# Early loads regrouped, and another order of the filter and back steps, in a spectral and attention kernel

## The chip, the cores and the metric

The kernel runs on one core of a Trainium2 chip. The metric is the device time of one execution in microseconds (us). The profile is of one execution on the same kind of core, in which every instruction of the engines and every packet of the DMA engines has a time. The engines are PE (TensorE, the matmuls), ACT (ScalarE), DVE (VectorE), POOL (GpSimd) and SP (SyncE, which here only issues transfers). Each of them works through its own instructions in order.

## What is computed

Four layers follow one another, each added to its input x (2048 rows by 512 columns, bfloat16): a spectral filter, attention, the same filter, the same attention.

```python
def _A_ref(x, w_r, w_i):
    X = rfft2(x.astype(float32), axes=(-2, -1))
    X = X * (w_r + 1j * w_i)
    return irfft2(X, s=(S, D), axes=(-2, -1)).astype(bfloat16)
...
x = x + _A_ref(_layernorm(x), A_w_r, A_w_i)
x = x + _B_ref(_layernorm(x), B_wq, B_wk, B_wv, B_wo)   # attention, 32 heads of 16, one key and value head
x = x + _A_ref(_layernorm(x), A_w_r, A_w_i)
x = x + _B_ref(_layernorm(x), B_wq, B_wk, B_wv, B_wo)
```

## The kernel before

`full_kernel` (L1162) loads x in four quarters into `x_sb`, and between them the tables `PH`, `S1` and `C1`, all on SP's queue. Then it runs twice `spectral_layer` (L217) and `attention_layer`. The change is in the loads of `full_kernel` and in `spectral_layer`.

The spectral layer makes the two-dimensional transform of matrix products with tables of sines and cosines. It works on two halves h of the frequencies, 0 and 1, in these steps:

- `forward(k, h)` (L257) multiplies two row tiles of x, turned by transposes (L198) in the first layer, with half h of `PH`: the transform along the columns. ACT scales the result by the layer norm's factor, which DVE (`norm.stats`, L155, called by `feed`, L1211) and POOL (L161) make.
- `first(k, h)` (L268) multiplies with `C1`, `S1` and `S1N` (the negated `S1`, made by DVE at L1220), copies the result to `A1`, and stores it to DRAM (`D1`, L277).
- `cross1(g, h)` (L279) reads it back in another order into `A2` (L280).
- `filtered(j)` (L317), called f below, multiplies a part of `A2` with the table `G`, copies it by ACT to X (L326), and multiplies it on DVE with the weights `wr_sb` (L330) and `wi_sb` (L332). `joined()` (L337) makes Z of the two products (L342, L343); it is called inside the next `filtered`, between its two products. There are eight, j = 0 to 7; 0 to 3 belong to half 0, 4 to 7 to half 1, and f4 is the first that reads half 1 of `A2`.
- `back(j)` (L345), called b, multiplies Z with the tables `H1`, `H2`, `H2N`, copies the result to B1 and stores it to DRAM (`D2`, L355).
- `cross2(h, g)` (L357) reads it back into `B2` (L358): four transfers for each half. Those of half 0 are called x0 below.
- `along(q, h)` (L374, L379) and `last(t, h)` (L388) are the inverse transform along the columns, with the addition to x; at the end of the layer attention's first keys and queries are made (L450), and L425 is its last line.

The loops `for k in range(9 + behind)` (half 0) and `for k in range(9)` (half 1) interleave forward, first and cross1. Inside them `load(k)` (L235) puts the loads of the layer's weights and tables into the queues at a given step: `wr_sb` at step 3, `H2` at 4 and `H1` at 5 on POOL's queue, `wi_sb` at 6, `G` at 9 where it is not loaded yet. The order of instructions on PE, ACT, DVE and SP is that of the program inside `spectral_layer` (`tc.manual_schedule`); POOL's is not fixed, and its instructions run as early as their data and the tile framework's order allow. A transfer that waits on SP's queue holds up every transfer behind it. The first four readings of half 0 and the stores of `D1` and `D2` are all on this queue. `wr_sb` shares its memory with the keys `Kv` of the attention layer before it (`tag="wrkv"`), `wi_sb`, `H1` and `H2` lie in a pool that is opened for each spectral layer, in memory which attention's pools used before.

The order of filter and back steps (L361) was f0, f1, f2, b0, f3, b1, f4, b2, f5, b3, f6, b4, x0, f7, b5, b6, b7, in both spectral layers.

Of the kernel before, what the change touches and what calls it, by code (L numbers as in the profile page):

```python
# [11 lines left out]
P = 128  # L12
BF = mybir.dt.bfloat16
# [32 lines left out]
VCELLS = 128  # L46
LASTW = 6
NEGATE = 7
NORMED, NORMG = (1,), ((3,), (3,), (3,))
OUTK, LATE_AT = 2, 4  # L50
TWICE = ((7,), 8)
# [87 lines left out]
def tile_of(x, k):  # L139
    return x[:, k // 4, k % 4, :]  # L140
# [69 lines left out]
def rotate(nc, ps, c, s, sn, re_im, first):  # L210

    nc.tensor.matmul(ps, lhsT=c, rhs=re_im, start=True, stop=False, skip_group_check=True)  # L212
    nc.tensor.matmul(ps[:, 0:128], lhsT=s, rhs=re_im[:, 128:256], start=False, stop=False, skip_group_check=True)
    nc.tensor.matmul(ps[:, 128:256], lhsT=sn, rhs=re_im[:, 0:128], start=False, stop=True, skip_group_check=True)  # L214


def spectral_layer(nc, tc, tabs, ht, A_w_r, A_w_i, x_sb, bigp, pre, norm, att, feed, weights):  # L217
    C1, S1, S1N, PH, ident = (tabs[n] for n in ("C1", "S1", "S1N", "PH", "ident"))
    with tc.tile_pool(name="workA", bufs=2) as work, tc.tile_pool(name="tabA", bufs=1) as tabA, \
# [7 lines left out]
        wi_sb = tabA.tile([P, 16, 256], BF, name="wi_sb")  # L227
        H1, H2, H2N = (tabA.tile([P, 16, P], BF, name=f"tab_{n}") for n in ("H1", "H2", "H2N"))

        def tables(names):  # L230
            for name in names:
                if tabs[name] is None:
                    tabs[name] = ht.load(tabs["pool"], name)

        def load(k):  # L235

            if k == 3:
                nc.sync.dma_start(out=wr_sb, in_=A_w_r.rearrange("(p a) f -> p a f", p=P)[:, :, 1:NF])
            elif k == 6:
                nc.sync.dma_start(out=wi_sb, in_=A_w_i.rearrange("(p a) f -> p a f", p=P)[:, :, 1:NF])  # L240
            elif k == 9:
                tables(("G",))
            elif k == 4:
                ht.load(tabA, "H2", H2, eng=nc.gpsimd)
            elif k == 5:
                ht.load(tabA, "H1", H1, eng=nc.gpsimd)
            elif k == 19:
                tables(("CS", "PSC", "PSS", "hmask"))
            weights(k)
# [29 lines left out]
        def cross1(g, h):  # L279
            nc.sync.dma_start(out=A2[32 * g:32 * g + 32, h, :, :],  # L280
                              in_=D1[h, 4 * g:4 * g + 4, :, :].rearrange("t (a b) c -> (t a) b c", b=16))
# [3 lines left out]
        for k in range(9 + behind):  # L285
# [6 lines left out]
            at = k - behind  # L292
# [7 lines left out]
        for k in range(9):  # L300
# [5 lines left out]
            if k >= 4 and k % 2 == 0:  # L306
                cross1((k - 4) // 2, 1)
            if k == NEGATE:
                nc.vector.tensor_single_scalar(out=H2N, in_=H2, scalar=-1.0, op=ALU.mult)
        cross1(3, 1)  # L310
        load(19)
        G, CS, PSC, PSS = (tabs[n] for n in ("G", "CS", "PSC", "PSS"))
# [4 lines left out]
        def filtered(j):  # L317

            h, b4 = j // 4, 4 * (j % 4)
            hf = slice(128 * h, 128 * h + 128)  # L320
            X = work.tile([P, 4, 2, 128], BF, name="X", tag="X", bufs=3)
            for b in range(b4, b4 + 4, 2):
                ps = bank()
                for i in range(2):
                    rotate(nc, ps[:, i, :], G[:, 0, :], G[:, 1, :], G[:, 2, :], A2[:, h, b + i, :], i == 0)
                nc.scalar.copy(out=X[:, b - b4:b - b4 + 2, :, :], in_=ps.rearrange("p j (r f) -> p j r f", r=2))  # L326
            m1, m2 = (M[:, i, j % 4] for i in range(2))
            wrb = wr_sb[:, b4:b4 + 4, hf].unsqueeze(2).to_broadcast([P, 4, 2, 128])
            wib = wi_sb[:, b4:b4 + 4, hf].unsqueeze(2).to_broadcast([P, 4, 2, 128])
            nc.vector.tensor_tensor(out=m1, in0=X, in1=wrb, op=ALU.mult)  # L330
            joined()
            nc.vector.tensor_tensor(out=m2, in0=X, in1=wib, op=ALU.mult)  # L332
            products.append((j, m1, m2))
# [11 lines left out]
        def back(j):  # L345
            h, b4 = j // 4, 4 * (j % 4)
            for b in range(b4, b4 + 4, 2):
                ps = bank()
                for i in range(2):
                    rotate(nc, ps[:, i, :], H1[:, b + i, :], H2N[:, b + i, :], H2[:, b + i, :], Z[:, h, b + i, :], i == 0)  # L350
                if j == 7 and b > b4:
                    nc.vector.tensor_copy(out=B1[:, h, b:b + 2, :], in_=ps)
                else:
                    nc.scalar.copy(out=B1[:, h, b:b + 2, :], in_=ps)
                nc.sync.dma_start(out=D2[h, :, b:b + 2, :], in_=B1[:, h, b:b + 2, :])  # L355
# [2 lines left out]
            eng.dma_start(out=B2[:, h, 4 * g:4 * g + 4, :],  # L358
                          in_=D2[h].rearrange("(t a) b c -> t (a b) c", t=16)[4 * g:4 * g + 4].rearrange("t m c -> m t c"))

        for j in range(10):  # L361
            if j < 8:
                filtered(j)
            if j >= 7:
                joined()
            if j >= 2:
                back(j - 2)
            if j == 6:
                for g in range(4):
                    cross2(0, g, nc.sync)  # L370

# [789 lines left out]
@with_exitstack  # L1161
def full_kernel(ctx, tc, A_x, A_w_r, A_w_i, B_x, B_wq, B_wk, B_wv, B_wo, out):  # L1162
    nc = tc.nc
    const = ctx.enter_context(tc.tile_pool(name="const", bufs=1))
    x_v = A_x.flatten_outer_dims().rearrange("(p r t) d -> p r t d", r=R, t=T)
    x_sb = const.tile([P, R, T, 512], BF, name="x_sb")
    ht = Tables(nc)
    tabs = dict(pool=const, CS=None, PSC=None, PSS=None, hmask=None, G=None)
    tabs["ident"] = ht.load(const, "ident", eng=nc.scalar)
    for part in (slice(0, 2), slice(2, 4)):  # L1170
        nc.sync.dma_start(out=x_sb[:, 0, part, :], in_=x_v[:, 0, part, :])
    tabs["PH"] = ht.load(const, "PH")
    tabs["S1"] = tabs["C1"] = None
    for r in range(1, R):
        nc.sync.dma_start(out=x_sb[:, r, :, :], in_=x_v[:, r, :, :])
        if r < 3:
            for n in ("S1", "C1"):
                tabs[n] = ht.load(const, n, tabs[n], slice(8 * r - 8, 8 * r))
    mhalf = const.tile([P, 4], F32, name="mhalf")
    nc.gpsimd.memset(mhalf, -0.5)  # L1180
    tabs["S1N"] = const.tile([P, 16, P], BF, name="tab_S1N")
    wq_sb = const.tile([P, NC, D], BF, name="wq_sb")
    wk_sb = const.tile([P, NC, DH], BF, name="wk_sb")
    wka = const.tile([P, NC, 8, DH], BF, name="wka")
    wo_sb = const.tile([P, 4, D], BF, name="wo_sb")
    wv_sb = const.tile([P, NC, DH], BF, name="wv_sb")
    xn_sb = const.tile([P, R, T, 512], BF, name="xn_sb")
    lnpool = ctx.enter_context(tc.tile_pool(name="lnpool", bufs=1))
    bigp = ctx.enter_context(tc.tile_pool(name="bigp", bufs=6))
    out_v = out.flatten_outer_dims().rearrange("(p r t) d -> p r t d", r=R, t=T)  # L1190
    att = Attention(nc, tabs, const, bigp, lnpool, wq_sb, wka.rearrange("p c v d -> p c (v d)"), wv_sb, xn_sb)

    def weights(k):
        if k == 19:
            nc.sync.dma_start(out=wk_sb, in_=B_wk.rearrange("(c p) j -> p c j", p=P))
            nc.sync.dma_start(out=wv_sb, in_=B_wv.rearrange("(c p) j -> p c j", p=P))
            for v in range(8):
                nc.gpsimd.tensor_copy(out=wka[:, :, v, :], in_=wk_sb)
        elif k == 20:
            nc.sync.dma_start(out=wq_sb, in_=B_wq.rearrange("(c p) j -> p c j", p=P))  # L1200
            nc.sync.dma_start(out=wo_sb, in_=B_wo.rearrange("(g p) c -> p g c", p=P))

    def make_norm():
        return Norm(nc, lnpool, mhalf, x_sb, xn_sb)

    def store(k, eng=nc.sync):
        eng.dma_start(out=tile_of(out_v, k), in_=tile_of(x_sb, k))

    norm = make_norm()

    def feed(k, psum):  # L1211

        for t in (0, 1) if k == 0 else ():
            norm.stats(t, tile_of(x_sb, t))
        if k < 7:
            norm.stats(2 * k + 2, tile_of(x_sb, 2 * k + 2))
            norm.stats(2 * k + 3, tile_of(x_sb, 2 * k + 3))
        if k in (2, 5):
            part = slice(0, 8) if k == 2 else slice(8, 16)
            nc.vector.tensor_single_scalar(out=tabs["S1N"][:, part], in_=tabs["S1"][:, part], scalar=-1.0, op=ALU.mult)  # L1220

    feed.busy, feed.xT = True, []
    for layer in range(2):
        norm_in, norm_out = make_norm(), make_norm()
        spectral_layer(nc, tc, tabs, ht, A_w_r, A_w_i, x_sb, bigp, norm, norm_in, att, feed,
                       weights if layer == 0 else lambda k: None)
        feed = attention_layer(nc, tc, att, norm_in, norm_out, x_sb, wo_sb, None if layer == 0 else store)
        norm = norm_out
# [47 lines left out]
```

## Time and profile before

| what | us |
|---|---|
| three timed runs | 1409.14, 1414.59, 1416.40 (median 1414.59) |
| the profiled execution | 1412.01 |
| its span, first to last instruction | 1410.20 |
| first spectral layer, to its last line L425 | 0 to 96.2 |
| first attention layer | 96.3 to about 709 |
| second spectral layer | about 709 to 793.9 |
| second attention layer | 793.9 to the end |

PE is busy in 95%, ACT in 94%, DVE in 93% of the span; the mean granted clock of PE is 0.997 of full speed. The DMA engines moved 34.5 MB, most of it in the two spectral layers. A row of the timeline gives the start, the duration, the engine, the line, the operation, the tile written and the tiles read, and in brackets how long the engine had been idle before it and what ended this. A row of the chain of waits gives start, duration and what was waited for. An engine's name with a q is its queue of transfers, the row being the issue and not the transfer.

### The profile page before, as it was taken

To read this page: it belongs to the slowest core of one execution; us is meant where nothing else is said; L and a number is where in the kernel's file an instruction comes from. 1 tells how busy PE (TensorE), PEld (TensorE's weight loads), DVE (VectorE), ACT (ScalarE), POOL (GpSimd) and SP (SyncE) were. 2 spreads that over 40 slices of the span, in tenths; PEclk is the share of its full clock that TensorE was granted. 3 is DMA by queue.
4 is the path that set the end of the run, shared out by engine and by line. 5 is a ranking of instruction groups with operands and counts; after the bars stand their busy time and mean duration, and the time that the engine had idled before them with its cause. 6 is when DMAs were issued, how large, how long until landed. Compare 5 with 4: busy or idle time off the path is not lost.

```text
span 1410.2 us, 34818 instructions
## 1 busy us (share of the span) xinstructions
PE 1344.2 (95%) x14050; PEld 471.8 (33%) x14118; DVE 1310.5 (93%) x2271; ACT 1331.1 (94%) x1542; POOL 824.6 (58%) x483
## 2 busy tenths in 40 slices
PE   7799999999999999999997999999999999999998
PEld 6653232223222222222275422332222222222222
DVE  5679999999999999999966899999999999999997
ACT  5679999999999999999955899999999999999997
POOL 2125676667666667667610267666666666666664
PEclk9999999999999999999999999999999999999999
DMA  7700000000000000002064000000000000000000
GB/s 249 210 29 2 1 2 2 2 1 2 2 2 1 2 2 2 1 1 40 8 183 147 2 2 2 2 1 9 5 5 1 6 9 5 2 1 10 9 2 16
DMA packets 44770, 34.52 MB, mean 24 GB/s; under 512 B 10048, under 2 KB 42048, under 8 KB 44096
## 3 DMA queue, kind: packets, MB, share of 16 engines
q1 hardware_dynamic: 41632, 28.98, 7.2%
q8 instruction: 110, 1.80, 0.5%
q0 software_dynamic: 576, 2.10, 0.4%
q10 hardware_dynamic: 2400, 1.21, 0.3%
q14 instruction: 52, 0.43, 0.1%
HBM read 20.22 MB, written 10.49 MB: 22 GB/s over the span
## 4 chain that ended last, share of the span: by engine, by line
ACT 47%; PE 33%; issue 9%; DVE 7%; DMA 3%; POOL 0%; SPq 0%; DVEq 0%; ACTq 0%; POOLq 0%
ACT e L1077 46%; PE pv L866 13%; PE sc L911 11%; DVE ph L951 3%; PE aux L911 2%; PE ps L262 1%; DMA D<-A 1%; PE aux L450 1%; DVE ln_stats L155 1%; DVE ph L983 1%; PE ps L212 1%; DMA x_sb<-in_A_x_dram 1%; DMA B<-D 1%; PE pv L881 1%; PE aux L679 1%
## 5 line engine op out<-in xcount | busy, mean ns | idle before, releaser
L1077 ACT ACTIVATE e<-sc 128x1024 bf16<-128x1024 f32 x1328 | 1218.2, 1166 | 2.9 <-PE sc L911 2.9
L975 POOL TENSOR_TENSOR ph<-ph,step 128x1024 int32<-128x1024 int32 x404 | 762.8, 1891 | 413.1 <-DVE ph L983 293.0
L951 DVE TENSOR_SCALAR ph<-aux 128x512 uint16<-128x512 f32 x1440 | 904.0, 679 | 20.5 <-PE aux L911 15.9
L866 PE MATMUL pv<-ph,vaug 128*32 128x512 bf16 x4320 | 548.8, 386 | 0.7 <-POOL ph L975 0.3
L911 PE MATMUL sc<-QT,Kv 32*128 32x512 bf16 x2656 | 521.8, 380 | 23.5 <-ACT e L1077 16.2
L866 PE MATMUL pv<-e,vaug 128*32 128x512 bf16 x2656 | 483.9, 384 | 0.3 <-ACT e L1077 0.3
L911 PE MATMUL aux<-QT,Kv 32*128 32x512 bf16 x1440 | 455.8, 384 | 1.0 <-DVE ph L951 0.5
L911 PEld LDWEIGHTS <-Kv 32*128 32x128 bf16 x4096 | 183.4, 91 | 525.9 <-issue 517.6
L881 PE MATMUL pv<-wo_sb,zeros 128*32 128x512 bf16 x1200 | 257.8, 383 | 0.0
L866 PEld LDWEIGHTS <-vaug 128*32 128x32 bf16 x6976 | 147.6, 94 | 292.8 <-issue 281.6
L983 DVE TENSOR_SCALAR ph<-ph 128x2048 uint16<-128x2048 uint16 x316 | 216.5, 685 | 0.5
L161 POOL TENSOR_TENSOR ln_rstd<-ln_veps,mhalf 128x4 f32<-128x4 f32 x16 | 16.6, 1036 | 123.7 <-DVE ln_veps L160 123.6
L155 DVE BATCH_NORM_STATS2 ln_stats<-x_sb 128x6 f32<-128x512 bf16 x64 | 43.5, 680 | 28.1 <-ACT x_sb L413 19.4
L881 PEld LDWEIGHTS <-zeros 128*32 128x32 bf16 x1200 | 60.1, 94 | 1.9 <-issue 0.3
L781 DVE STREAM_TRANSPOSE oT<-pv 128x512 f32<-128x512 f32 x64 | 45.2, 707 | 9.2 <-PE pv L866 9.2
L184 ACT ACTIVATE Pk<-ps,ln_rstd 128x256 bf16<-128x256 f32 x64 | 26.8, 474 | 21.9 <-PE ps L262 19.0
L262 PE MATMUL ps<-tab_PH,xT 128*128 128x256 bf16 x256 | 35.3, 286 | 3.9 <-DMA tab_PH<-const_PH 3.0
L276 DVE CAST A<-ps 128x512 bf16<-128x512 f32 x28 | 19.2, 689 | 17.8 <-PE ps L214 17.8
L450 PE MATMUL aux<-xTa,wq_sb 128*128 128x512 bf16 x90 | 32.6, 384 | 2.8 <-issue 2.4
L803 POOL TENSOR_TENSOR on<-oT,rden 128x512 bf16<-128x512 f32 x30 | 31.7, 1056 | 2.0 <-DVE rden L807 1.8
L679 PE MATMUL aux<-wo_sb,ph 128*128 128x512 bf16 x72 | 26.1, 383 | 3.6 <-issue 2.1
L262 PEld LDWEIGHTS <-xT 128*128 128x128 bf16 x256 | 25.1, 102 | 8.1 <-issue 3.7
(109 smaller groups left out, 668.3 us busy)
## 6 DMA issues: line engine op xcount, KB each, us to landing
D<-A SPq DMA_DIRECT2D x32, 128.0 KB, 3.2
A<-D SPq DMA_DIRECT2D x16, 256.0 KB, 3.5
D<-B SPq DMA_DIRECT2D x32, 128.0 KB, 2.5
B<-D SPq DMA_DIRECT2D x12, 256.0 KB, 4.5
tab_H<-const_H POOLq DMA_DIRECT2D x4, 512.0 KB, 6.4
wr_sb<-in_A_w_r_dram SPq DMA_DIRECT2D x2, 1024.0 KB, 6.2
wi_sb<-in_A_w_i_dram SPq DMA_DIRECT2D x2, 1024.0 KB, 7.4
out_dram<-x_sb SPq DMA_DIRECT2D x15, 128.0 KB, 1.7
```

The source lines that it names most:

```text
L155: nc.vector.bn_stats(st, src)
L262: nc.tensor.matmul(ps[:, j, :], lhsT=xT[:, cc, 2 * k + j, :], rhs=PH[:, cc, 256 * h:256 * h + 256], start=(cc == 0), stop=(cc == NC - 1), ...
L450: self.nc.tensor.matmul(ps, lhsT=w(c), rhs=self.xTq[:, c, qc * 512:(qc + 1) * 512], start=(c == 0), stop=(c == NC - 1), skip_group_check=True)
L679: nc.tensor.matmul(ps, lhsT=OTs[qb][:, g4, kk * P:(kk + 1) * P], rhs=wo_sb[:, g4, :], start=first, stop=last, skip_group_check=True)
L781: end = clock.now(clock.FLIP, lambda: nc.vector.transpose(out=oT[:, par].rearrange("p b c -> p (b c)"), in_=pv), clock.last + clock.MM_END)
L866: nc.tensor.matmul(pv_tiles[gi][32 * i:32 * i + 32, :], lhsT=vaug[:, kc, j, :], rhs=es, start=((gi, i) not in started), stop=(left[gi, i] ...
L881: nc.tensor.matmul(pv_tiles[gi][32 * i:32 * i + 32, :], lhsT=att.zeros, rhs=wo_sb[:, 0, :], start=False, stop=False, skip_group_check=True)
L911: nc.tensor.matmul(out, lhsT=Kv[r, par, kc * P:(kc + 1) * P], rhs=QT[r, g, qb * 512:(qb + 1) * 512], start=True, stop=True, skip_group_che ...
L951: end = clock.now(clock.Z, lambda: nc.vector.tensor_scalar(out=z.bitcast(U16), in0=ps, scalar1=SCALE * LOG2E * 128.0, scalar2=127.0 * 128. ...
L975: nc.gpsimd.tensor_tensor(out=copy.bitcast(I32), in0=z.bitcast(I32), in1=step.to_broadcast([P, w // 2]), op=ALU.add)
L983: nc.vector.tensor_scalar(out=one.bitcast(U16), in0=z.bitcast(U16), scalar1=float(PHASE[1]), scalar2=None, op0=ALU.add)
L1077: nc.scalar.activation(out=e[:, 0:ng * 512], in_=sc[:, 0:ng, :].rearrange("p a b -> p (a b)"), func=ACT.Exp, scale=SCALE)
```

## The change

The early loads: `PH` comes in two halves, the first in its old place, the second behind all of x. In the first layer `wr_sb`, `wi_sb`, `H2` and `H1` are put into SP's queue at steps 3, 4, 6 and 8, `H2` and `H1` no longer into POOL's. In the second layer all four are put into SP's queue at step 0, ahead of the layer's first store. The order of the filter and back steps is written out as a string: b2 and b3 and the four readings of half 0 come ahead of f4, and a join of its own ahead of b3.

```diff
+STEPS = "f0 f1 f2 b0 f3 b1 b2 j3 b3 x0 f4 f5 f6 b4 f7 b5 j7 b6 b7"
...
+        first_layer = tabs["G"] is None
...
         def load(k):
 
-            if k == 3:
+            at = (3, 4, 6, 8) if first_layer else (0, 0, 0, 0)
+            if k == at[0]:
                 nc.sync.dma_start(out=wr_sb, in_=A_w_r.rearrange("(p a) f -> p a f", p=P)[:, :, 1:NF])
-            elif k == 6:
+            if k == at[1]:
                 nc.sync.dma_start(out=wi_sb, in_=A_w_i.rearrange("(p a) f -> p a f", p=P)[:, :, 1:NF])
-            elif k == 9:
+            if k == at[2]:
+                ht.load(tabA, "H2", H2)
+            if k == at[3]:
+                ht.load(tabA, "H1", H1)
+            if k == 9:
                 tables(("G",))
-            elif k == 4:
-                ht.load(tabA, "H2", H2, eng=nc.gpsimd)
-            elif k == 5:
-                ht.load(tabA, "H1", H1, eng=nc.gpsimd)
             elif k == 19:
                 tables(("CS", "PSC", "PSS", "hmask"))
             weights(k)
...
-        for j in range(10):
-            if j < 8:
+        for step in STEPS.split():
+            j = int(step[1])
+            if step[0] == "f":
                 filtered(j)
-            if j >= 7:
+            elif step[0] == "b":
+                back(j)
+            elif step[0] == "j":
                 joined()
-            if j >= 2:
-                back(j - 2)
-            if j == 6:
+            else:
                 for g in range(4):
                     cross2(0, g, nc.sync)
...
-    tabs["PH"] = ht.load(const, "PH")
+    tabs["PH"] = const.tile([P, 4, 512], BF, name="tab_PH")
+    ph = nc.inline_tensor(ht.host["PH"], name="const_PH").ap()
+    nc.sync.dma_start(out=tabs["PH"][:, :, 0:256], in_=ph[:, :, 0:256])
...
         if r < 3:
             for n in ("S1", "C1"):
                 tabs[n] = ht.load(const, n, tabs[n], slice(8 * r - 8, 8 * r))
+    nc.sync.dma_start(out=tabs["PH"][:, :, 256:512], in_=ph[:, :, 256:512])
```

## The prediction

> **What bounds the kernel now.** I read first the busy shares in forty slices. Slices of 35 us are full on PE, DVE and ACT except at 0 to 105 us, about 705 to 810 us and the last slice: between them the attention stages keep ACT busy, and the change touches no line of theirs. So only the two spectral stages (L217 to L425) count: 0 to 95 us ("S1") and 709 to 793 us ("S2"). In the chain of waits, S1 begins with a load:
>
> ```profile
> 2.12 9.83 DMA x_sb<-in_A_x_dram
> 11.97 0.70 DVE ln_stats L155
> ...
> 41.76 3.72 DMA D<-A
> 45.92 2.79 DMA tab_CS<-const_CS
> ...
> 61.96 3.51 DMA D<-B
> 65.54 3.42 DMA B<-D
> ```
>
> The reader is to see that transfers end four waits: the second quarter of x; the exchange of the second half of A through DRAM (the row naming tab_CS is the queue's place: f4's operand is A2, landed at 48.74); the store and the reading of the second half of B. The timeline shows what happens at the first wait and at f4, first in S1, then in S2:
>
> ```profile
> 2.31 0.76 POOL L135 DMA_DIRECT2D tab_H<-const_H  x1
> 11.97 0.69 DVE L155 BATCH_NORM_STATS2 ln_stats<-x_sb 128x6 f32<-128x512 bf16 x1 [4.47 <-DMA x_sb<-in_A_x_dram]
> ```
> ```profile
> 48.98 0.27 PE L212 MATMUL ps<-A,tab_G 128*128 128x256 bf16 x1 [1.17 <-DMA tab_CS<-const_CS]
> ```
> ```profile
> 746.53 0.37 PE L212 MATMUL ps<-A,tab_G 128*128 128x256 bf16 x1 [2.96 <-DMA A<-D]
> ```
>
> S2 waits longer, and its clock falls. Busy time by stretch (PE is the second number; the clock is the last but two):
>
> ```profile
> 43.39:46.80 3.41, 1.83 (x25) 1.74 (x26) 3.41 (x9) 1.93 (x5) 0.00 (x0) 1.00 0.73 201
> 67.28:70.69 3.41, 1.44 (x10) 0.91 (x11) 0.00 (x0) 1.03 (x2) 0.00 (x0) 1.00 1.08 295
> 70.69:74.10 3.41, 3.41 (x11) 1.51 (x10) 1.70 (x4) 2.32 (x5) 0.00 (x0) 0.50 0.88 278
> 743.12:746.53 3.41, 0.45 (x8) 0.29 (x6) 1.96 (x4) 1.32 (x3) 0.00 (x0) 1.00 0.74 227
> 746.53:749.94 3.41, 3.41 (x25) 2.89 (x26) 0.90 (x2) 1.75 (x3) 0.00 (x0) 0.50 0.06 13
> ```
>
> The halved stretches begin 675.84 us apart, 198 times 3.413 us: the clock is set on a fixed grid, and follows the stretch before: 1.44 us of PE work in 3.41 was too little, 1.83 was enough.
>
> **Part 1, the start (S1).** Gone from the first microseconds: H2 and H1, which POOL issues at 2.3 and 3.2. Their packets (256 of 4 KB at 0.165 us, over 16 DMA engines) take 2.64 us of each engine between 6.7 and 12.3. PH, 8 packets of 159 ns on each engine (1.27 us), becomes a half of 32 packets of 512 bytes, at the 27 ns that such packets take in wr_sb's load: 0.86 us. So 0.41 us goes there too. Of the sixteen parts of x's second quarter fourteen landed by 8.49, the last two at 10.71 and 11.95. If those two stay late: 11.95 - 2.64 - 0.41 = 8.9, a gain of 3.1. If they keep up, x lands near 7, and DVE is free of the first quarter's statistics at 7.5: a gain of 4.5. I take the middle, **3.8**.
>
> The Trainium skill, "DMA: Bandwidth & Descriptors", Latency and other measured facts, says that two of the engines are usually slow and guesses that POOL's descriptors do it; by that guess the gain would be 4.5, and the sum below 0.7 better. The row for it is only the two late parts.
>
> What is late next: DVE, nearly without a pause from 11.97 to 26 (sixteen statistics at 0.66 to 0.69, copies, the negated table). S1's and C1's first halves landed at 13.1 and 13.8, 1.2 and 1.8 after x in the same queue, so move with it; x's last quarter (17.6, needed at 22) has slack, and PH's second half (0.86 us of DMA, needed at 29.6) too. The weights and H now stand in SP's queue at steps 3, 4, 6 and 8, each an issue of 0.43 to 0.66 us, with the stores of A behind them. I cost this at nothing: the last exchange of half 0 was issued by 35.7 and f0 starts at 40.5; in the new order wr and wi (landing 6.1 and 6.7 apiece) are through by about 27, H and the last stores by 31. Without that cover each late microsecond is one on f0.
>
> **Part 2, the order of steps.** A step is 0.88 us on PE (12 matmuls), 0.96 on ACT (two copies), a filter 2 x 0.605 on DVE, its join 2 x 0.335. b2 and b3 now come before f4. PE takes b2 when Z2 is there (49.1) and b3 when Z3 is (50.4, its join now before m1 of f4), so f4 starts at 51.3 instead of 48.98. Its wait is gone, but DVE needs f4's copies, which now come at 53.1 instead of 50.74 and idles 2.8 us. From there DVE paces: four filters and joins, 7.5 us plus small waits, and Z7 is ready at 61.3 instead of 59.73. **b7 ends 1.6 to 1.7 us later in S1**, by the same list that gives the old order within 0.2 us. This is the edit's price where A2 was late by only 1.17.
>
> In S2 A2 came at 746.5, 10.2 us after f0 (S1: 8.2). b2 and b3 fit before that, so f4 starts about then, warm, and b7's last copy ends 22.75 us after f0, as in S1's list. f0 itself waited 0.51 and starts at 735.75, because the four loads, now ahead of every store of A, are through before the first exchange is due: Kv is last read at 706.2, H's tiles were free at 708.95, and 3 MB take 2 x 3.5 + 2.64 us, to about 720; that exchange is issued at 721.95. Last copy 758.5, instead of 760.48: 2.0 gained.
>
> **Part 3, the readings x0.** 1 MB in 1 KB packets (64 per engine at 47 ns, 3 us) were issued at 56.89 to 58.91, with the last stores of B behind them; the last store took 3.51 where the median is 2.5. In the new order they go out by 57.3 while b4's first store comes at 57.2: nothing is blocked, and the last store has a free queue. Bounds: no gain, or 1.0; I take 0.7 in S1. In S2, from the last copy to the first reading of B took 7.89 us, in S1 7.44; new 6.7, so 1.2 there.
>
> **The clock.** PE stood idle 2.09 us before L379 at 69.01, and the half clock after it cost S1 25.91 us from there to L425, against S2's 24.23: 1.7. In the new order PE reaches that wait 1.6 later and the reading comes 0.9 later, so the idle is about 1.4, below the 1.58 that the row with 1.83 had: 1.7 goes. S2's half clock is within its 2.0.
>
> The Trainium skill, "TensorE: Matmul & The Clock Gate", What's actually happening, lets the clock fall after a whole idle window. The row with 1.44 us of work speaks against it. By the page the new gaps of part 2 could cost nothing; by the row they can, which is a rival below.
>
> **The sum.** Start -3.8; S1 +1.6 - 0.7 - 1.7 = -0.8; S2 -2.0 - 1.2 = -3.2; together **-7.8 us**. The profiled execution took 1412.01 (span 1410.20), so it would take 1404.2. The three timed runs are 1409.14, 1414.59 and 1416.4; with the profiled one their median is 1413.3, and I give **1405.5** as the time, 9 under the median shown. About 0.5% (7.1 us) is what a measurement here can tell from no change, so the forecast lies just beyond that bound.
>
> **Rivals.**
> 1. *The small version.* The two late parts stay late (-3.1), the order's price in S1 stays whole and its clock still falls (+1.7), S2 gains only 2.0: -3.4, 1409.9. For it: the clock grid is met by chance, and why two DMA engines lag is not shown. Against: x0 does leave the stores' way. Chance 0.32.
> 2. *The clock falls in the filter stage.* New PE gaps: 1.9 us from f6 to b4, and 1.4 + 0.4 around b2; a stretch that holds them whole has 1.5 to 1.6 us of work, between 1.44 (fell) and 1.83 (kept). Price up to 1.7 in each stage: -7.8 + 3.4 = -4.4, 1408.9. Chance 0.10.
> 3. *Slower: the first forward step waits for both halves of PH.* They are one tile; if the wait goes by tile, PE stands until the second half lands: x's last quarter landed at 17.57, less 2.64 and 0.41, plus 0.86, is 15.4. The first matmuls of L262 start there, not at 8.91; those, the transposes and the second eight take 4.6, and the first rotation starts at 20.0, not 14.53: +5.5 in place of -3.8, in all +1.5, 1414.8. It decides once that landing is past 10.1: with 1.9 us of matmuls behind it, PE would come to its next transposes after 12.0, where it began them before. Against: the second forward step starts at 12.82 while ACT writes other slices of xT at 13.07, so waits follow slices. Chance 0.05.
> 4. *More.* Start -4.5, the stores -1.0 in S1, S2 -4.2: -11, 1402. For it: fourteen parts of x land early. Chance 0.08.
>
> The forecast has 0.45, with its own range of 1402.5 to 1408.5. **Range** 1400.5 to 1412: from the fourth rival with the timed runs' scatter to the second and first with it; left out are the slower case and the edges. **Chances**: beyond 0.5% faster (below 1407.5) four fifths of the forecast and the fourth rival, 0.36 + 0.08, with some runs of the first and second, 0.47; slower by over 0.5% only if the third is worse than priced, 0.04; within, 0.49.
>
> **What would show it.** Right: the second DVE wait for x ends near 8 and f0 starts near 36.7; b2 and b3 before f4 in both stages; DVE idle some 2.8 us before f4's first product in S1; f4 in S2 without a DMA wait and at full clock; the last store of B landing in 2.5 us. Wrong: the first L262 waiting for tab_PH past 10.1 us; a clock of 0.50 among f4 to b7; f0 waiting for A2; SP's stores of A in S2 issued later than 712.56 by more than a microsecond. The forecast fails mostly if the start gains little or the two stages' ends do not follow b7.

## The result and the profile after

Nine runs of the changed kernel have a median of 1406.32 us (1404.63 to 1408.3), nine of the kernel before 1413.68 (1409.14 to 1416.97): a ratio of 0.9953, 95% interval 0.9938 to 0.9968. The profiled execution after took 1406.89 (span 1405.1), that of before 1412.01: the two profiles are 5.1 us apart, the medians 7.4.

In the changed file the lines of the spectral layer stand one to five further down (L212 is L213, L262 is L266, L326 is L330, L379 is L384, L425 is L430). The chain of waits of the kernel after, first spectral layer (start, duration, what was waited for):

```profile
2.30 6.94 DMA x_sb<-in_A_x_dram
...
43.01 2.99 DMA D<-A
46.06 4.48 DMA A<-D
...
62.99 3.17 DMA D<-B
66.28 3.41 DMA B<-D
```

The same four transfers end the same waits. x landed 2.7 us earlier (9.24 for 11.95), but the last two rows end at 69.69, where the chain before ended its reading at 68.96: by then the new order of steps has cost more than was left of the early start. The timeline of the kernel after at these places:

```profile
9.26 0.69 DVE L156 BATCH_NORM_STATS2 ln_stats<-x_sb 128x6 f32<-128x512 bf16 x1 [1.76 <-DMA x_sb<-in_A_x_dram]
39.22 0.27 PE L213 MATMUL ps<-A,tab_G 128*128 128x256 bf16 x1 [0.76 <-DMA D<-A]
50.59 0.28 PE L213 MATMUL ps<-A,tab_G 128*128 128x256 bf16 x1 [0.26 <-DMA A<-D]
52.39 0.69 DVE L334 TENSOR_TENSOR M<-X,wr_sb 128x1024 bf16<-128x1024 bf16 x1 [3.18 <-ACT X L330]
69.74 1.05 PE L384 MATMUL ps<-tab_CS,B 128*128 128x256 bf16 x8 [1.87 <-DMA B<-D]
745.45 0.27 PE L213 MATMUL ps<-A,tab_G 128*128 128x256 bf16 x1
747.29 0.69 DVE L334 TENSOR_TENSOR M<-X,wr_sb 128x1024 bf16<-128x1024 bf16 x1 [2.80 <-ACT X L330]
```

Row two is f0, which now waits for a transfer; row three f4 in S1, four is DVE at f4's product; the sixth is f4 in S2, with no bracket: its wait of 2.96 is gone. The busy time by stretch, on the grid of the clock, around f4 in S1 and in S2:

```profile
51.96:55.38 3.42, 1.66 (x24) 1.41 (x22) 2.99 (x6) 2.36 (x5) 2.96 (x6) 1.00 0.77 254
...
744.86:748.28 3.42, 3.40 (x47) 3.06 (x44) 0.99 (x2) 3.10 (x8) 0.00 (x0) 1.00 0.46 153
748.28:751.69 3.41, 1.78 (x24) 1.68 (x24) 3.41 (x9) 2.06 (x5) 0.00 (x0) 1.00 0.62 185
```

From 17.8 us on, up to the last 1.5 us, no stretch is at half clock; before, two were, counted from 19.5 us on. Ahead of these times PE runs at half speed in both profiles. The clock column does not show it: it reads 1.00 at the start as well. The durations of eight equal matmuls of L266 do; in the kernel after:

```profile
14.51 1.92 PE L266 MATMUL ps<-tab_PH,xT 128*128 128x256 bf16 x8
17.88 1.04 PE L266 MATMUL ps<-tab_PH,xT 128*128 128x256 bf16 x8
```

This first rise of the clock came between 8.0 and 20.2 us in the fourteen profiles of this document. A stretch of the grid with 2.68 us of work (4.17 to 7.58) and the two after it did not raise the clock here. In the run with the old order in S2 alone (below), whose program in S1 is the changed kernel's, the grid lay otherwise: the stretch from 5.62 held 2.80 us of work, and full speed came behind it, at 9.03:

```profile
6.71 1.87 PE L267 MATMUL ps<-tab_PH,xT 128*128 128x256 bf16 x8 [0.61 <-DMA tab_PH<-const_PH]
9.14 1.04 PE L267 MATMUL ps<-tab_PH,xT 128*128 128x256 bf16 x8
```

Where the 5.1 us went, from the starts of the first L262 (L266) row of S2 and of the last matmuls of the layer:

| stretch | before | after | difference |
|---|---|---|---|
| start to the first matmul of S2 (S1 and attention) | 709.23 | 708.22 | -1.0 |
| from there to the last L425 (L430) matmuls | 83.20 | 79.30 | -3.9 |
| from there to the end of the span | 617.8 | 617.6 | -0.2 |

### The profile page after: what moved, and what is told of

Same layout as the page of the kernel before. It is cut to its first block, busy times and chain, and to the rows that moved or that the text cites. A ratio compares the mean times of both kernels' runs of the same rounds, so it can differ in the third digit from the quotient of the medians.

```text
span 1405.1 us, 34816 instructions
## 1 busy us (share of the span) xinstructions
PE 1341.5 (95%) x14050; PEld 470.6 (33%) x14118; DVE 1310.0 (93%) x2271; ACT 1330.8 (95%) x1542; POOL 822.7 (59%) x479
## 4 chain that ended last, share of the span: by engine, by line
ACT 48%; PE 33%; issue 9%; DVE 7%; DMA 3%; SPq 0%; POOL 0%; DVEq 0%; ACTq 0%
ACT e L1082 47%; PE pv L871 13%; PE sc L916 10%; DVE ph L956 3%; PE aux L916 2%; PE ps L266 2%; DVE ln_stats L156 1%; PE aux L455 1%; PE ps L213 1%; DMA B<-D 1%; DVE ph L988 1%; PE pv L886 1%; PE aux L684 1%; DMA x_sb<-in_A_x_dram 0%; DMA D<-B 0%
## 5 line engine op out<-in xcount | busy, mean ns | idle before, releaser
L185 ACT ACTIVATE Pk<-ps,ln_rstd 128x256 bf16<-128x256 f32 x64 | 26.8, 472 | 19.7 <-PE ps L266 15.2
L266 PE MATMUL ps<-tab_PH,xT 128*128 128x256 bf16 x256 | 35.3, 286 | 1.6 <-DVE oT L786 0.8
L213 PE MATMUL ps<-Z,tab_H 128*128 128x256 bf16 x64 | 15.1, 275 | 13.0 <-DVE Z L347 12.9
```

Of the source, the lines that this page charges most:

```text
L266: nc.tensor.matmul(ps[:, j, :], lhsT=xT[:, cc, 2 * k + j, :], rhs=PH[:, cc, 256 * h:256 * h + 256], start=(cc == 0), stop=(cc == NC - 1), ...
```

## The experiments

Two questions were open. First, which edits make the gain: the theory was that S2's part is the one that counts, and that S1's earlier start is lost again at the exchange of A; the rival was the prediction's own sum, with half of the gain from the start. Second, what decides that the clock falls.

All times are beside runs of the kernel before on the same chip, whose medians were 1413.56 (first four kernels), 1413.27 (next four), 1412.93 (next three) and 1412.62 (the last).

### One part of the change at a time

**The order alone** (loads as before):

```diff
-        for j in range(10):
+        for step in STEPS.split():
```

> The kernel before with the new order of steps alone, in both spectral layers; the loads stay as they were. Theory (the order costs where A2 is only a little late and gains where it is very late): in the first layer the last copy of b7 comes 22.8 to 23.3 us after f0 instead of 21.1, and the first reading of the second half of B about 1 us later than 69.0; in the second layer f4 no longer starts at half clock, b7's last copy comes about 2 us and the reading about 3 us earlier. In all -1 to -4 us, ratio 0.997 to 0.999. Rival (the order gains in both layers, because the four readings of half 0 leave the way of the last stores): the first layer's reading of B also comes earlier, in all -5 us or more. Second rival (the second layer's gain came from the loads): the second layer gains under 1 us and the whole is +0.5 to +2.

1407.54 us (1404.98 to 1407.9), ratio 0.9956, 0.9944 to 0.9968. The order alone gives nearly the whole gain: 6.0 us, where the theory had 1 to 4. S2 took 79.96 from its first matmul to its end, f4 there had no wait, and from 11 us on no stretch was at half clock in either layer:

```profile
746.76 0.27 PE L213 MATMUL ps<-A,tab_G 128*128 128x256 bf16 x1
```

In S1 the first reading of half 1 of B came at 69.68, 0.7 later than before, as the theory had it, although f0 started 2.9 earlier (37.61) with the loads unchanged. Part of what the theory missed is the clock: it is 1.0 in all five runs (see the end of this section).

**The early loads of S2 alone** (old order, PH whole, S1's loads as before):

```diff
+            elif k == 0:   # second layer only: wr_sb, wi_sb, H2, H1 on SP's queue
```

> The kernel before with the second spectral layer's four loads at step 0 on SP's queue, nothing else changed (the first layer's loads, H2 and H1 on POOL's queue among them, the old order). Theory (SP's queue was held up by stores behind wr_sb and wi_sb): f0 of the second layer loses its wait of 0.51 us, the second half of A2 lands about 8 to 9 us after f0 instead of 10.2, f4 starts some 1.5 us earlier relative to f0, and the clock perhaps does not fall; counted from the layer's first matmul of L262, the first reading of the second half of B comes 2 to 4 us earlier. In all -2 to -4 us, ratio 0.997 to 0.9985. Rival (the loads only move the waits, the order made the gain): below 1 us.

1409.92 (1405.36 to 1414.02), 0.9976, 0.9965 to 0.9987. S2 took 79.85, although a stretch of it was at half clock. Timeline, f4 and the first readings of B in S2:

```profile
743.48 0.27 PE L212 MATMUL ps<-A,tab_G 128*128 128x256 bf16 x1
...
759.64 2.43 PE L387 MATMUL ps<-tab_CS,B 128*128 128x256 bf16 x16 [1.97 <-DMA B<-D]
```

With the loads ahead of the stores, the exchange of A is done before f4 even in the old order. The order and the loads thus take away the same wait: 83.2 becomes 80.0 by the one, 79.9 by the other, 79.3 by both. What the loads alone leave is the new wait in the second row: x0 comes too late for readings that now start earlier.

**The loads of S1 alone**, and **PH in halves alone**:

```diff
+            elif k == 4:   # first layer only: wr_sb at 3, wi_sb at 4, H2 at 6, H1 at 8 on SP's queue
```

> The kernel before with the first spectral layer's loads of wr_sb, wi_sb, H2, H1 at steps 3, 4, 6, 8 on SP's queue, PH whole, the second layer as before, the old order. Theory (H gone from the start brings x earlier, but the weights then stand ahead of A's exchange): the second quarter of x ends DVE's wait near 9.6 instead of 11.97, the second half's matmuls begin 2 us earlier, but f0 waits for A2 and starts at 39.0 to 39.6 instead of 40.51, and f4 waits about 2 us and starts at 50 to 51 instead of 48.98: the whole is +1 to -0.5 us. Rival (the prediction as it was: the loads have cover): f0 near 38 without a wait, f4 near 46.5, in all -2 to -2.5 us.

```diff
-    tabs["PH"] = ht.load(const, "PH")
+    nc.sync.dma_start(out=tabs["PH"][:, :, 0:256], in_=ph[:, :, 0:256])
```

> The kernel before with PH in two halves alone: the first half in PH's old place, the second behind all of x. Theory (a half has 32 packets of 0.027 us on each DMA engine instead of 8 of 0.159): the first matmuls of L262 start some 0.5 to 1 us before 8.91, the second quarter of x ends its wait 0.3 to 0.6 us before 11.97, and the whole gains as much, -0.3 to -0.6 us, which the timing cannot tell from nothing. Rival (the small packets cost more than their bytes): x comes no earlier or later, 0 to +0.5 us.

1413.46 (ratio 0.9999, 0.999 to 1.0008) and 1412.94 (0.9997, 0.9989 to 1.0006): neither does anything. The timelines show why; f4 in S1, with S1's loads early and then with PH in halves:

```profile
49.03 0.37 PE L212 MATMUL ps<-A,tab_G 128*128 128x256 bf16 x1 [3.09 <-DMA A<-D]
```
```profile
48.15 0.27 PE L212 MATMUL ps<-A,tab_G 128*128 128x256 bf16 x1 [2.59 <-DMA tab_CS<-const_CS]
```

f0 came at 38.65 and 38.26 in place of 40.51, and f4 at 49.03 and 48.15 where it was at 48.98: the wait for half 1 of A took most or all of what the start gained (1.17 before, 3.09 and 2.59 now). With the wait the clock fell, at 48.0 and 48.5. How much of the gain at f0 is the edits' is open: in the kernel before with idle matmuls (below), whose loads are the old ones, f0 came at 38.91, and with PH in halves the first L262 started at 9.54, later than the 8.91 of before and not 0.5 to 1 earlier. In S2, which neither edit touches, f4 waited 3.22 and 3.35.

### What holds S1: a place in the queue, or bytes

**H later in S1**, behind the exchange of half 0:

```diff
-            at = (3, 4, 6, 8) if first_layer else (0, 0, 0, 0)
+            at = (3, 4, 11, 12) if first_layer else (0, 0, 0, 0)
```

> The changed kernel with S1's loads of H2 and H1 behind half 0's exchange (steps 11 and 12 in place of 6 and 8); S2 and the order as changed. Theory (the exchange of half 1 of A through DRAM sets the fifth product of the filter in S1, which started at 48 to 51 us in all six profiles whatever the start did): first product f0 at 37.5 to 40.5, f4 at 48 to 51, first reading of half 1 of B at 69 to 71, time within 1.5 us of the changed kernel's 1406.3. Rival (the two tables lie in SP's queue ahead of half 0's exchange and hold it): the exchange of half 0 lands 1 to 2 us earlier, f0 near 37.5, f4 and the end of S1 earlier by the same, 1404 to 1405.

1407.96 (1406.09 to 1410.74), 0.9967, 0.9955 to 0.998: not the 1404 to 1405 of the rival. f0 came at 37.27, f4 at 51.96 after a wait of 1.31, the first reading of half 1 of B at 72.02. The same megabyte, moved from half 0's exchange to half 1's, would delay that one, which fits these rows; they lie outside the theory's bounds too (48 to 51, 69 to 71). The span's first 95 us had two stretches at half clock, and the profiled execution was the slowest of the eleven (1410.74).

**S1's loads on ScalarE's queue**:

```diff
+            eng = nc.scalar if first_layer else nc.sync
-                nc.sync.dma_start(out=wr_sb, ...
+                eng.dma_start(out=wr_sb, ...
```

> The changed kernel with S1's four loads issued on ScalarE's queue in place of SP's, at the same steps. Theory (the bytes of the exchange bound S1, not the place of the loads in SP's queue): f4 at 48 to 51, first reading of half 1 at 69 to 71, time within 1 us of the changed kernel's 1406.3. Rival (stores of half 0 stand behind the loads in SP's queue): f0 1 to 2 us earlier than 39.2, S1's end earlier, 1404.5 to 1405.5; or ScalarE's issues delay its copies, 0.3 to 0.6 slower.

1405.04 (1402.63 to 1406.55), 0.9944, 0.9929 to 0.9959; f0 at 38.15, f4 at 49.82. The interval holds the changed kernel's ratio, so no gain over it is shown. The time and f0 lie in the rival's bounds, f4 and the first reading of half 1 (69.12) in the theory's, so this run alone does not tell the two apart.

**One megabyte less.** The load of the weights' imaginary part is left out in S1, where the real part is multiplied twice:

```diff
-            if k == at[1]:
+            if k == at[1] and not first_layer:
-            wib = wi_sb[:, b4:b4 + 4, hf]...
+            wib = (wr_sb if first_layer else wi_sb)[:, b4:b4 + 4, hf]...
```

> The changed kernel without the load of the weights' imaginary part in S1: the filter of S1 multiplies by the real part twice, with the same instructions. 1 MB less goes through the DMA queues between 18 and 28 us, where the changed profile has a DMA share of 0.78 to 1.11. Theory (S1's start gain of about 2 us is held by TensorE until 42 us and then lost because the exchange of A shares full DMA engines with the loads): DMA share in 21 to 28 well under 1, no DMA wait ahead of f0, f0 at 36.7 to 37.6, f4 at 47.5 to 49, S1's end 92 to 93 in place of 94.0, time 1404.3 to 1405.3. Rival (the exchange takes its time by itself, store and reading one behind the other, whatever else is moved): f0 38 to 39, f4 near 50, time within 0.6 of the changed kernel's 1406.3.

1402.95 (1402.07 to 1403.96), 0.9935, 0.9916 to 0.9954: faster than the theory's bounds. The right neighbour for its S1 is the kernel with the old order in S2 alone (below), whose S1 is the changed kernel's, whose x landed at the same time, 8.34 against 8.35, and whose clock rose early too, at 9.03 against 8.22. Busy time from 21 to 28 us, with the load and without (the DMA share is the last number but one):

```profile
21.00:28.00 7.00, 6.38 (x63) 5.27 (x61) 2.15 (x4) 5.18 (x12) 1.01 (x1) 1.00 1.07 292
```
```profile
21.00:28.00 7.00, 6.38 (x63) 5.27 (x61) 2.15 (x4) 5.18 (x12) 1.01 (x1) 1.00 0.76 227
```

Every engine does the same, and only the DMA share differs, 1.07 against 0.76. Then f0, again with the load and without:

```profile
37.64 0.27 PE L214 MATMUL ps<-A,tab_G 128*128 128x256 bf16 x1 [1.88 <-DMA D<-A]
```
```profile
35.62 0.27 PE L213 MATMUL ps<-A,tab_G 128*128 128x256 bf16 x1
```

f0 comes 2.0 earlier, f4 2.0 (46.57 for 48.59), the last matmuls of S1 2.6 (89.23 for 91.84). So a megabyte of load in SP's queue at this time costs about 2 us where PE is early enough to wait for the exchange. Whether its bytes or its place in the queue cost this is not separated, since the edit takes away both. The row that bears on it is the issue of the last reading of half 0 of A, with the loads on SP's queue, with the same bytes on ScalarE's queue, and with one megabyte less:

```profile
34.04 0.32 SPq L285 DMA_DIRECT2D A<-D  x1
```
```profile
31.92 0.32 SPq L285 DMA_DIRECT2D A<-D  x1
```
```profile
31.18 0.32 SPq L284 DMA_DIRECT2D A<-D  x1
```

On ScalarE's queue the exchange was nearly as early with every byte in it; the first load was issued there at 11.27, on SP's queue at 13.86, behind the first store. f0 did not profit, because PE, at half clock from 14.87 to 18.28 in that profile, came to it only at 38.15. In the profile of the changed kernel too it was mostly PE that held f0: it worked without a pause from 26.8 us on, and the wait that followed was 0.76.

### The order in each layer, and the clock

**The old order in S1 alone**:

```diff
-        for step in STEPS.split():
+        for step in (OLD if first_layer else STEPS).split():
```

> The changed kernel with the old order of filter and back steps in S1 alone. Theory (in S1 the new order gives only the stretch at half clock and little more): DMA wait ahead of f4 of 2 to 4 us as in the kernel before and in the two runs with the old order, a fall of the clock within 4 us of f4 or at the reading of half 1, and S1's end 0.5 to 2 us later: 1407 to 1408.5. Rival, the prediction's own price (the new order itself costs 1.6 in S1, and only the kept clock pays for it): S1's end 1.6 earlier where the clock stays, level where it falls: 1404.7 to 1406.3.

1407.27 (1405.19 to 1409.95), 0.9963, 0.9951 to 0.9976. The profiled execution had no stretch at half clock and reached S2 at 706.79, 1.4 before the changed kernel; two runs at full clock took 1405.2 and 1405.3, four at a mean clock of 0.998 from 1407.0 to 1410.0. f4 waited 2.53, as expected, but this time the grid of the clock spared it: no stretch there had little enough work. The time alone agrees with the theory, the best runs with the prediction's price.

**The kernel before, with matmuls that do nothing**, eight into an unused bank ahead of the readings of half 1 of B:

```diff
+        fill = psum.tile([P, 512], F32, name="ps", tag="pa")
+        for _ in range(8):
+            nc.tensor.matmul(fill, lhsT=ident, rhs=PSC[:, 0, :], start=True, stop=True, skip_group_check=True)
```

> The kernel before, with eight matmuls into an unused bank ahead of the readings of half 1 of B, in both layers; they compute nothing that is used. Theory (the clock falls because TensorE stood still for about 2 us there, and the fall costs about 1.7 in S1): in S1 no half clock at 69 to 73, from the first reading to the end of S1 24.2 in place of 25.9; in S2 the fall at f4 (746.5) stays, since it is ahead of the matmuls added; time 0.5 to 1.7 below the kernel before's 1413.6. Rival (a fall there is a matter of phase, and a stretch at half clock elsewhere takes its place, or the fall costs nothing): within 0.4 of the kernel before. If the eight matmuls reach past the landing of half 1, each 0.2 us over is lost in both layers: up to 1 slower.

1409.6 (1407.37 to 1413.42), 0.9981, 0.9971 to 0.9992: 3.7 faster, twice the bound that the theory gave. S1 had no half clock from 69 to 73 and took 24.07 from its first reading of half 1 (67.79) to its last matmuls (91.86), where it took 25.75 before; in S2 the fall at f4 stayed (744.9), as expected. One stretch explains 1.7 of the 3.7. In the profile f0 came 1.6 earlier too (38.91), with the same loads; the rest is not explained.

**The old order in S2 alone**, with x0 behind b3:

```diff
+OLD = "f0 f1 f2 b0 f3 b1 f4 b2 f5 b3 x0 f6 b4 f7 j7 b5 b6 b7"
+        for step in (STEPS if first_layer else OLD).split():
```

> The changed kernel with the old order of filter and back steps in S2 alone, the first half's exchange moved up there to behind b3 (before: behind b4); loads and S1 as changed. From first product of S2 to its end the profiles had 83.2 before, 79.3 changed, 79.9 with the early loads and the old order (with one stretch at half clock in it, at 760.9, where the first half's readings waited 1.97). Theory (in S2 the order and the loads take away the same wait, that of f4 for half 1 of A, 2.96; given the early loads the new order is worth nothing there): S2 lasts 78 to 79.5, f4 without a DMA wait, time within 1 us of the changed kernel's 1406.3. Rival (the new order is worth the 2.0 that the prediction put on b7's last copy, which the loads do not give): S2 lasts 81, 1408 to 1408.5.

1404.92 (1403.67 to 1406.87), 0.9949, 0.9933 to 0.9966. S2 took 78.38 and f4 had no wait: given the early loads, the new order is worth nothing in S2. (The same order and loads in S2 left f4 a wait of 1.73 in the last run below, so f4 is not always covered.)

**The old order in S1, with matmuls that keep the clock** ahead of f4 (eight) and of the readings (six):

```diff
+S1STEPS = "f0 f1 f2 b0 f3 b1 w0 f4 b2 f5 b3 f6 b4 x0 f7 j7 b5 b6 b7"   # w0: fill(8)
+        if first_layer:
+            fill(6)
```

> The changed kernel with the old order in S1 alone and, in S1, eight matmuls into an unused bank ahead of f4 and six ahead of the readings of half 1 of B, whose results are not used. Theory (the old order is the shorter one in S1 by the 1.6 of the prediction, and loses it only by stretches at half clock at f4 or at the readings): no half clock between 40 and 75, mean clock 1.0 in most runs, S1's end near 92.5, 1404.3 to 1405.5, less scatter than the old order without them (1407.3, 1405.2 to 1410). Rival (the falls of the clock cost nothing, the old order is level with the new one): 1406 to 1407.5 whatever the clock. If the eight reach past the landing of half 1 of A, f4 is up to 0.5 later.

1406.38 (1404.35 to 1407.61), 0.9957, 0.9942 to 0.9972, the clock 1.0 in three of six runs. The profiled execution, the fastest of the six, reached S2 at 705.87, 2.3 before the changed kernel, but the median is the changed kernel's: the rival's time, the theory's profile. At full clock four profiles with the old order in S1 reached S2 at 705.87 to 706.79 (mean 706.35), three with the new one at 706.25 to 708.22 (707.5). The order's price in S1 is 1.2 by this, with identical S1 programs 2.0 apart. Those two differ in the first rise of the clock (17.82 and 9.03). Three profiles with the old order and the new loads whose clock rose at 16.4 to 17.1 reached S2 at 706.4 in the mean, the changed kernel's at 708.22: a price of 1.8, from one profile on its side. The timed runs do not show it.

**The parts that came out best, together** (old order in both layers, loads of S1 on ScalarE's queue, fills in S1):

> The parts that came out best together: S1 with the old order, the matmuls that keep the clock as in the run above and its four loads on ScalarE's queue; S2 with the early loads of the changed kernel, the old order and the first half's exchange behind b3. Theory: S1's end near 92, S2 78 to 79.5, 1402.5 to 1404.5. Rival (the loads on ScalarE's queue were only a matter of clock, 1.0 in five of six runs): the time of the run above, 1404.3 to 1405.5; or, if the old order in S2 is worse by 2.0, 1406.

1405.21 (1402.79 to 1407.05), 0.995, 0.9934 to 0.9966: level with each of its parts, in the rival's bounds. S1's last matmuls came at 92.17, and S2 took 79.55. No version of the changed kernel that computes the whole is shown to be faster than it; all their intervals overlap its own.

**The clock, over all profiles.** In the fourteen profiles, the spectral layers (from 20 us on) were cut into the 3.413 us stretches of each profile's own grid (edges rounded to 0.01). Of the twelve stretches at full clock with the least work on PE (0.44 to 1.53 us) eleven were followed by a stretch at half clock; one with 1.47 was not. Of the hundreds with 1.55 us or more none was. From three kernels (loads on ScalarE's queue; one megabyte less; old order in S2), the rows next to the border, the first with the stretch that follows:

```profile
45.60:49.01 3.41, 1.52 (x19) 1.29 (x20) 2.73 (x6) 2.15 (x5) 0.00 (x0) 1.00 0.79 209
49.01:52.42 3.41, 3.41 (x28) 2.91 (x26) 0.03 (x1) 2.34 (x4) 1.46 (x8) 0.50 0.72 241
```
```profile
49.19:52.60 3.41, 1.55 (x22) 1.32 (x21) 3.41 (x7) 1.86 (x5) 2.73 (x6) 1.00 0.34 111
52.60:56.01 3.41, 2.25 (x29) 1.80 (x27) 3.13 (x8) 2.32 (x5) 0.00 (x0) 1.00 0.83 232
```
```profile
756.56:759.97 3.41, 1.47 (x7) 0.49 (x5) 0.00 (x0) 0.00 (x0) 0.00 (x0) 1.00 0.42 125
759.97:763.38 3.41, 2.58 (x18) 1.60 (x19) 0.27 (x1) 1.96 (x4) 0.00 (x0) 1.00 0.70 183
```

What counts is the work within one stretch of the grid, and the border lies near 1.5 of 3.41 us. The way up has another border: from half clock, a stretch with 2.38 us of work did not raise the clock (the run with S1's loads alone stayed there from 48.0 to 54.8), and of the first stretches of the profiles none with up to 2.78 us did, while all with 2.80 or more did. The old order has waits of 1.2 to 3.4 us at f4 and near 2 at the readings, and whether one of them leaves a stretch below the border is a matter of where the grid lies in that run. The new order leaves 1.66 us or more in every stretch of the changed kernel's profile, which fits its better clock. It does not keep the clock at every position of the grid: with the same order in S1 the clock fell at 49.02 in the run with the loads on ScalarE's queue (the first pair of rows), and at 42.56 and 73.28 in the run with H later.

The timed runs fit this. One stretch at half clock lowers the mean granted clock of a run by 0.0012 (1.7 of some 1405 us). The 76 runs of the kernel before beside the experiments have a mean of 0.997, which is some 2.5 stretches; the changed kernel's nine 0.999, the order alone 1.0 in each of five. A line through all 187 runs, each kernel's own mean taken out, gives 0.87 us for each 0.001 (0.70 to 1.05). The difference of 0.002 goes with 1.7 us of the 7.4. (The half speed of the first 8 to 20 us is not in these means.)

## Why the prediction was right

The time, 1406.32 against 1405.5, and the sum, -7.4 by the medians against -7.8, were right; the largest term was not, and the closeness of the sum is in part luck. By the two profiles the terms come to -1.3 for the start, +2.2 for the order, -0.2 for x0 and -1.7 for the clock in S1, -3.9 in S2 and -0.2 behind it: -5.1. The rest of the -7.4 lies in other runs than the two profiled ones, in part in their clock, and the prediction did not count it.

- **The start, -3.8: failed.** f0 came 1.3 earlier (39.22, not 36.7), and neither S1's loads alone nor PH in halves alone changed the time. Three steps took the rest. First, x landed 2.7 earlier, not 3.8, with four parts of its quarter late (8.69 to 9.24); the size is uncertain, since kernels with POOL's loads had it between 9.44 and 11.97. Second, the prediction leaves out the half clock at the start: PE's second forward step was 2.7 ahead (10.12 for 12.82), but full speed came only 1.7 earlier (17.82 for 19.49), and from there to the last forward step PE was 2.2 ahead. Third, the weights and H in SP's queue were costed at nothing, with the cover "the last exchange of half 0 was issued by 35.7 and f0 starts at 40.5". That cover holds only for an f0 at 40.5: the last reading of half 0 was issued by 36.0, no earlier than before, f0 waited 0.76 for it, and the DMA share from 21 to 28 us was 1.11. The prediction gave this price itself ("each late microsecond is one on f0") and named the wait as a sign of being wrong. The run with 1 MB less showed how large it gets when PE is early: 2.0 at f0 and 2.6 at S1's end.
- **The order in S1, +1.6: the mechanism right, the size between 1.2 and 2.2.** b7's last copy came 23.3 after f0 (22.75 forecast, 21.1 before), DVE stood idle 3.18 ahead of f4's product (2.8), and f4 still waited 0.26 for a transfer. That is 2.2 by the two profiles, 1.2 by the mean of those at full clock.
- **x0 out of the last store's way, -0.7: measured -0.2.** That store took 3.17 in place of 3.51, not 2.5; from the last copy to the first reading 7.23 for 7.44, -0.2. Why the store stays slow with x0 out of its way was not tried.
- **The clock in S1, -1.7: right in size, wrong in reason.** From the first reading to the layer's last matmuls it took 24.07 for 25.75. But PE's idle was 1.87, not 1.4; with 2.12 in the run with S2's loads alone the clock fell, with 2.26 in the order alone it did not. It is the work in a stretch of the grid, as the prediction's own rows had it, not the length of one idle time, and whether a stretch falls below the border there is in part luck.
- **S2, -3.2: measured -3.9.** f4 without a wait and warm, the last copy 22.67 after f0 (22.75 forecast) and 2.2 earlier from the start of S2 (2.0); from there to the first reading 6.21 for 7.89, -1.7 (-1.2 forecast), the last store 2.07. That the early loads alone would do nearly the same was not seen: the parts do not add.
- **The rest.** By the two profiles all differences come to -5.1. The other 2.2 of the medians lie in which runs were profiled: that of before is 1.7 under its runs' median, that of after 0.6 over. Of the runs' difference 1.7 goes with the clock, which the prediction counted once, in the one stretch of the profile.

Of the rivals, the small version had the right fate for the start, in part by its own cause (parts of x stayed late) and in part by others (the half clock at the start, the wait at f0). In the changed kernel's profile the clock did not fall in the filter stage; the least stretch had 1.66 us where 1.5 to 1.6 was feared. With the same order it did fall there in two other runs, so the second rival holds at some positions of the grid. The first forward step did not wait for the second half of PH: its first matmul started at 6.64.

The Trainium skill, "DMA: Bandwidth & Descriptors", Latency and other measured facts, names POOL's descriptors as its guess for two slow DMA engines. The profiles fit it in part: in the five kernels with POOL's loads in S1, x's second quarter was waited for until 9.44 to 11.97 (mean 10.8), in the nine without until 8.34 to 9.72 (9.1). But the loads' own bytes go with them, and some parts are late in both, so the cause isn't shown.

The Trainium skill, "TensorE: Matmul & The Clock Gate", What's actually happening, has a free-running window of 3413 ns, which the grid of every profile here agrees with (the two falls of before are 198 times 3.413 us apart), and a fall after an idle window. Here eleven windows that were not idle, with 0.44 to 1.53 us of work, were followed by one.

## What to carry to other kernels

A load in another engine's queue is not free where an exchange has to pass at the same time: here, with a DMA share of 1.07 from 21 to 28 us, a megabyte cost the step behind the exchange 2.0 us once PE was early enough to wait. Less to load brought the exchange forward, and so did the same loads in another queue, issued earlier. Where two edits take away the same wait (a load moved ahead, other work moved ahead), each alone can be worth nearly as much as both, so cost them together. A wait on PE has a second price, the clock, which depends on the work left in one stretch of a grid that the kernel doesn't control: judge an order by its least busy stretch at any position of the grid, and by many runs, since one profile shows one position. The same holds for the start: the durations of equal matmuls tell when full speed begins; here the clock column did not.

## What was not expected

- The border of the clock lies near 1.5 us of PE work in 3.413 us (11 of 12 stretches up to 1.53 fell, none from 1.55 up).
- Kernels with the same program in S1 reached S2 up to 2.0 us apart (708.22 and 706.25). Full speed began at 17.82 in the one and at 9.03 in the other, so the last forward step came 2.7 later in the first, and x landed later too (9.26 and 8.34): a single profile does not tell S1's variants apart, and neither did the timed runs of the last versions.
- Eight idle matmuls in the kernel before took 3.7 us off its time (0.9971 to 0.9992), more than the one stretch at half clock that they keep.
